# Splitting a weight transfer by tile, and moving the issue of attention's value loads

## The chip, the core and the metric

The kernel runs on one core of a Trainium2 chip. The metric is device time in microseconds (us), the median of several executions. The engines are TensorE (PE; PEld is its weight loads), VectorE (DVE), ScalarE (ACT), GpSimd (POOL) and SyncE (SP), which here issues all transfers from one queue, in order.

## What is computed

The result is a gated mix, `g * a + (1 - g) * b`, of an attention branch with memory and a gated feed-forward branch, over the same 2048 rows of 576 columns.

```python
x = A_x
g = _sigmoid((x * gate_w).sum(-1, keepdims=True))
a = _A_ref(x, A_wq, A_wk, A_wv, A_wo, A_beta)
b = _B_ref(x, B_w_gate, B_w_up, B_w_down)   # (gelu(x @ w_gate) * (x @ w_up)) @ w_down, F = 4608
return g * a + (1 - g) * b
...
for s in range(N):                          # N = 4 segments of 512 rows, 32 heads of 18
    logits = jnp.einsum("bhqd,bhkd->bhqk", qs, ks) * scale + mask
    a_dot = jnp.einsum("bhqk,bhkd->bhqd", _softmax(logits), vs)
    num = jnp.einsum("bhld,bhde->bhle", phi(qs), M)
    den = jnp.einsum("bhld,bhd->bhl", phi(qs), z)[..., None] + 1e-6
    outs.append(g * num / den + (1.0 - g) * a_dot)
    M = M + jnp.einsum("bhld,bhle->bhde", phi(ks), vs)
    z = z + jnp.einsum("bhld->bhd", phi(ks))
```

## The kernel before

The kernel holds each operand as a pair of float16 words, high and low, scaled by a power of two that is formed from sums of squares; most products are three matmuls. It has three stages.

**Projections.** The 2048 rows are four chunks of 512 (`s` or `c`, 0 to 3). The 576 columns of x are five tiles (`KT`; the fifth is a half tile). For each chunk nine column tiles of q and k (`project`, L329 in `chain_w`), and the value rows for four blocks of 128 rows (`vrows`, L339 in `chain_x`) are formed. They go to DRAM: q and k as `qk` from `stage` buffers, of which there are three (L485), values as `vp` (L510).

The first chunk's values don't wait for any scale: `first_words` (L527) multiplies the raw float32 x by the raw float32 value weights `raw_v`. The weights' 578 columns are two halves, `VB`: 288 columns (`NH`) and 290 (two more hold the mix's gate weight). For the first half all four row blocks are formed for k = 0 to 4, in the PSUM banks dn, dn, V and pv; for the second half row blocks 0 and 1 (banks G and U), then 2 and 3 (both st). `raw_v` and the raw q and k weights lie in memory that later is the accumulator `acc`, and so have that name in the trace.

Before and between these matmuls stand the sums that give the scales. `scale_x(0)` sums the squares of x, made by ACT (L154), with matmuls (L160), and reduces them on DVE (L162 to L169). `stat_v` sums the squares of each value tile, both halves, on DVE (L81). `scale_v` adds these with a matmul (L90) and so do the q and k sums later (`stat_qk`, on DVE L81 and ACT L431, then `scale_sum(0, ..)`, a second L90). With x's scale ACT makes high words (L175) and DVE low words (L180, L185).

**Attention and feed-forward together.** 72 steps (`step`) each take one of 36 tiles of 128 hidden columns for one pair of chunks; four steps make a block `fb`, the place in it is `i4`. `weights_load` issues the loads of gate and up words (`load_g`, L205, `raw`) and of down words (`load_d`, L211, `rawd`), four or five tiles ahead. In steps 2 to 65 a head of attention is worked on beside it: scores (L909), their maximum on DVE, powers and high words on ACT, low words on POOL, a transpose by DMA from `ph` to `pt` (L945), and the products with the values (`values`, L959). `load_v` (L882) loads the values of four heads as `vt`, of which there are two buffers.

**Tail.** The output projection and the mix.

The order on PE, DVE, ACT and POOL is that in which the code is written (`manual_schedule`). SP's order is chosen by the scheduler from what each transfer waits for. Transfers complete on eight lanes taken in turn (`DMAHW0` to `DMAHW7`); a transfer waits for the one before it on its lane, unless a wait before has covered that. The framework finds the waits between a transfer and its readers from the memory that each of them spans.

Of the kernel before, what the change touches and what calls it, by code (L numbers as in the profile page):

```python
# [24 lines left out]
NH = D // 2  # L25
KT = 5
# [16 lines left out]
def kernel(ctx: ExitStack, tc: tile.TileContext, xs, wqk, wv, wo, wgu, wd, beta, out):  # L43
    nc = tc.nc
    pe, act, dve, pool, sp = nc.tensor, nc.scalar, nc.vector, nc.gpsimd, nc.sync
# [19 lines left out]
    def flat(ap):  # L65
        return ap.rearrange("p a b -> p (a b)") if len(ap.shape) == 3 else ap

    def raw_tile():
        return wts.tile([P, 2 * KT * P], F32, name="raw", tag="raw", bufs=3)
# [72 lines left out]
    def load_first(raw_v):  # L142

        x_raw[0] = []
        x_sq[0] = flat(wts.tile([P, 2, GB * P], F16, name="pairg", tag="pairg", bufs=2)).bitcast(BF16)
        for k in range(KT):
            if k % 2 == 0:
                x_raw[0].append(raw_tile())
            sp.dma_start(x_raw[0][-1][:, (k % 2) * L : (k % 2 + 1) * L], xs[0, :, k])
            sp.dma_start(raw_v[:, k, :NH], wv[:, k, :NH])  # L150
        sp.dma_start(raw_v[:, :, NH:], wv[:, :, NH:])

    def square_x(c, k):
        act.activation(x_sq[c][:, k * L : (k + 1) * L], x_raw[c][k // 2][:, (k % 2) * L : (k % 2 + 1) * L], AF.Square)  # L154
# [47 lines left out]
    def load_g(f):  # L202
        if f < NF:
            raw_g[f] = raw_tile()
            sp.dma_start(raw_g[f], flat(wgu[f]))  # L205

    def load_d(f):
        if f >= NF:
            return
        raw_d[f] = home["r"].tile([P, D], F32, name="rawd", tag="rawd", bufs=2)  # L210
        sp.dma_start(raw_d[f], wd[f])  # L211
# [195 lines left out]
    with tc.tile_pool(name="prj", bufs=2, side="right", reuse_waits="tile") as pp:  # L407
# [12 lines left out]
        raw_v = kept["words"][:, : KT * (D + 2)].rearrange("p (k c) -> p k c", k=KT)  # L420
# [186 lines left out]
        with tc.manual_schedule(engines=ORDERED):  # L607
# [4 lines left out]
            for _ in range(30):  # L612
                pe.matmul(start[:, :P], onesb, onesb, start=True, stop=True)
            load_first(raw_v)
            for g in range(5):
                load_qk(g)
# [234 lines left out]
    with tc.tile_pool(name="keep", bufs=2, side="right", reuse_waits="tile") as kp, ExitStack() as tail:  # L851
# [25 lines left out]
        def load_v(gg):  # L877
            if gg >= H // 2:
                return
            hf, g = divmod(gg, H // 4)  # L880
            vts[gg] = ap_.tile([P, 8, 4 * VC], F16, name="vt", bufs=2)
            sp.dma_start(vts[gg], vps[hf][:, g * 4 * VC : (g + 1) * 4 * VC].rearrange("(t p) c -> p t c", p=P))  # L882
# [102 lines left out]
        def result_low(gg):  # L985
            hf, g = divmod(gg, H // 4)
            ob, oh = obs.pop(gg), ohs.pop(gg)
            dve.scalar_tensor_tensor(flat(oh[:, 1]), flat(ob), wsc[:, 3:4], flat(oh[:, 0]), OP.mult, OP.subtract)
            d0 = g * 4 * DH
            for i in range(2):  # L990
                for a, b, c in ((d0, min(d0 + 4 * DH, 4 * P), i * 4 * P), (max(d0, 4 * P), d0 + 4 * DH, (4 + i) * P - i * 64)):
                    if a < b:
                        sp.dma_start(oas[hf][:, c + a : c + b].rearrange("(t p) c -> p t c", p=P),
                                     oh[:, i, :, a - d0 : b - d0])
# [87 lines left out]
        def weights_load(fb, i4):  # L1082
            n0 = 2 * fb
            if i4 == 1:
                load_g(n0 + 4)
            if i4 == 2:
                load_d(n0 + 2)
            if i4 == 3:
                load_g(n0 + 5)
                if not fb:  # L1090
                    load_d(n0 + 3)
            if i4 == 0 and fb > 1:
                load_d(n0 + 1)
# [34 lines left out]
        def step(v):  # L1128

            f, p = divmod(v, 2)  # L1130
            fb, i4 = divmod(v, 4)
            c, e = 2 * p, 2 * p + 1
            k = v - LAG
# [56 lines left out]
            if fb:  # L1190
                weights_high(fb, i4)
                weights_low(fb, i4)
            weights_load(fb, i4)
            product(V, f, A22, x2_, 0, 4)
            rest(V, f, G4, x1, (0,) if fb else (0, 1))
# [82 lines left out]
            load_head(k + 2)  # L1278
            if done == H // 2 - 1:
                result_low(done)  # L1280
            if i4 == 0:
                load_v(fb)
            if i4 == 2:
                load_ob(fb)

# [31 lines left out]
        with tc.manual_schedule(engines=ORDERED):  # L1317
            for v in range(2 * NF):
                step(v)

                if v == LAST:
                    atn.close()
                    op_ = tail.enter_context(tc.tile_pool(name="outp", bufs=2, side="right", reuse_waits="tile"))
                if v >= LAST:
                    turned(2 * (v - LAST))
                    turned(2 * (v - LAST) + 1)
                    if v < LAST + 2:
                        finish(v - LAST)
# [4 lines left out]
            fb = NB - 1  # L1333
# [54 lines left out]
```

## Time and profile before

| | |
|---|---|
| time, median of 3 runs (lowest to highest) | 1606.44 us (1605.73 to 1607.4) |
| the profiled execution: time, span | 1604.73 us, 1603.0 us |
| mean granted TensorE clock | 0.998 |
| PE, DVE, ACT, POOL busy | 99%, 70%, 73%, 71% |
| moved by SP's queue | 206.92 MB, 71.6% of 16 DMA engines' time |

A busy time is an average over the stages. A wait is the idle time just before an instruction, with the instruction that ended last among those it waited for; a row of waits gives the sum, how often, and the longest. A chain row gives start, length and what ran. In a timeline row the start and the length come first, and the idle time before it, if any, stands last in brackets.

### The profile page before, as it was taken

To read this page: it belongs to the slowest core of one execution; us is meant where nothing else is said; L and a number is where in the kernel's file an instruction comes from. 1 tells how busy PE (TensorE), PEld (TensorE's weight loads), DVE (VectorE), ACT (ScalarE), POOL (GpSimd) and SP (SyncE) were. 2 spreads that over 40 slices of the span, in tenths; PEclk is the share of its full clock that TensorE was granted. 3 is DMA by queue.
4 is the path that set the end of the run, shared out by engine and by line. 5 is a ranking of instruction groups with operands and counts; after the bars stand their busy time and mean duration, and the time that the engine had idled before them with its cause. 6 is when DMAs were issued, how large, how long until landed. Compare 5 with 4: busy or idle time off the path is not lost.

```text
span 1603.0 us, 32556 instructions
## 1 busy us (share of the span) xinstructions
PE 1585.7 (99%) x11914; PEld 934.8 (58%) x11914; DVE 1117.5 (70%) x2938; ACT 1163.2 (73%) x1968; POOL 1134.0 (71%) x1093
## 2 busy tenths in 40 slices
PE   7999999999999999999999999999999999999999
PEld 5556654555555555555555555555555555555577
DVE  5755785777777777777777777677777777766643
ACT  4765554989888887879888888878798888864200
POOL 2231557788988888887979788888879797886300
PEclk9999999999999999999999999999999999999999
DMA  5632343879787887979797987989798979846241
GB/s 199 221 108 81 134 144 89 133 126 149 128 131 137 123 137 129 137 119 156 124 145 129 133 142 123 139 129 144 119 159 131 139 130 131 135 75 149 66 133 60
DMA packets 473248, 209.00 MB, mean 130 GB/s; under 512 B 427648, under 2 KB 438400, under 8 KB 472576
## 3 DMA queue, kind: packets, MB, share of 16 engines
q1 hardware_dynamic: 473088, 206.92, 71.6%
q8 instruction: 94, 1.54, 0.4%
q14 instruction: 66, 0.54, 0.1%
HBM read 90.99 MB, written 27.26 MB: 74 GB/s over the span
## 4 chain that ended last, share of the span: by engine, by line
PE 90%; ACT 3%; DMA 3%; POOL 2%; DVE 1%; issue 1%; SPq 0%; ACTq 0%; POOLq 0%; DVEq 0%
PE dn L1004 24%; PE U L1044 16%; PE V L1044 11%; PE G L1044 11%; PE pv L959 4%; PE st L339 3%; PE st L329 2%; PE dn L339 2%; PE U L1050 2%; PE G L329 2%; DMA pt<-ph 2%; PE G L1055 1%; PE V L1055 1%; PE st L909 1%; PE U L329 1%; PE G L1050 1%
## 5 line engine op out<-in xcount | busy, mean ns | idle before, releaser
L1004 PE MATMUL dn<-paird,hh 128*128 128x288 f16 x3396 | 485.4, 286 | 0.0
L939 POOL TENSOR_TENSOR ph<-pf,ph 128x512 f16<-128x512 f32 (+1 forms) x256 | 354.1, 1405 | 170.0 <-ACT ph L938 169.9
L1044 PEld LDWEIGHTS <-pairg 128*128 128x128 f16 x3024 | 279.8, 98 | 269.0 <-issue 18.3
L1004 PEld LDWEIGHTS <-hh 128*128 128x128 f16 x3456 | 338.0, 98 | 155.3 <-issue 0.2
L1012 DVE SCALAR_TENSOR_TENSOR acc<-dn,ev,acc 128x288 f32<-128x288 f32 x534 | 274.6, 515 | 69.0 <-PE dn L1004 68.7
L928 ACT ACTIVATE pf<-pf,mb,esc 128x512 f32<-128x512 f32 (+3 forms) x512 | 293.2, 644 | 7.0 <-POOL ph L939 0.4
L1044 PE MATMUL G<-x,pairg 128*128 128x512 f16 x864 | 220.9, 379 | 0.0
L1044 PE MATMUL U<-xt,pairg 128*128 128x512 f16 x864 | 210.0, 379 | 0.0
L1031 POOL TENSOR_TENSOR hh<-gl,hh 128x512 f16<-128x512 f32 x144 | 164.1, 1160 | 38.7 <-ACT hh L1030 38.7
L310 POOL TENSOR_TENSOR pairg<-raw,pairg 128x640 f16<-128x640 f32 (+2 forms) x144 | 174.5, 1235 | 12.9 <-ACT pairg L306 12.9
L938 ACT ACTIVATE ph<-pf 128x512 f16<-128x512 f32 (+1 forms) x256 | 172.7, 722 | 0.0
L306 ACT ACTIVATE pairg<-raw 128x640 f16<-128x640 f32 (+2 forms) x144 | 90.2, 653 | 107.9 <-POOL raw L300 56.0
L1198 DVE COPY gl<-U 128x512 f32<-128x512 f32 x72 | 49.8, 692 | 160.3 <-PE U L1044 157.4
L915 DVE CUSTOM_DVE_ANT_0 pf<-st,mask 128x512 f32<-128x512 f32 (+1 forms) x256 | 157.5, 616 | 0.0
L275 POOL TENSOR_SCALAR raw<-raw,sc 128x640 f32<-128x640 f32 x72 | 134.9, 1887 | 0.0
L1044 PE MATMUL U<-x,pairg 128*128 128x512 f16 x432 | 127.1, 379 | 0.4 <-DVE gl L1221 0.4
L1034 ACT ACTIVATE gl<-gl,sc 128x512 f32<-128x512 f32 x144 | 96.7, 716 | 41.8 <-DVE gl L1225 29.1
L915 DVE CUSTOM_DVE_ANT_0 pf<-dn,mask 128x256 f32<-128x256 f32 (+1 forms) x256 | 80.8, 354 | 60.5 <-PE dn L909 60.5
L1030 ACT ACTIVATE hh<-gl 128x512 f16<-128x512 f32 x144 | 85.9, 621 | 31.8 <-DVE gl L1026 31.3
L1044 PE MATMUL V<-xt,pairg 128*128 128x512 f16 x432 | 105.7, 381 | 0.0
L1044 PE MATMUL V<-x,pairg 128*128 128x512 f16 x432 | 104.8, 378 | 0.0
L959 PEld LDWEIGHTS <-pt 128*128 128x128 f16 x2560 | 78.4, 96 | 23.4 <-issue 16.3
(270 smaller groups left out, 2513.9 us busy)
## 6 DMA issues: line engine op xcount, KB each, us to landing
raw<-in_wgu_dram SPq DMA_DIRECT2D x36, 640.0 KB
rawd<-in_wd_dram SPq DMA_DIRECT2D x36, 288.0 KB
qk<-stage SPq DMA_DIRECT2D x36, 256.0 KB
qt<-qk SPq DMA_DIRECT2D x128, 72.0 KB
kt<-qk SPq DMA_DIRECT2D x128, 72.0 KB
vp<-vstage SPq DMA_DIRECT2D x16, 296.0 KB
vt<-vp SPq DMA_DIRECT2D x16, 296.0 KB
qt<-qk SPq DMA_DIRECT2D x128, 36.0 KB
```

Source lines behind the costliest of these rows:

```text
L275: pool.tensor_scalar(r, r, scl[f // 2][0][:, 0:1], None, OP.mult)
L310: pool.tensor_tensor(spot(f, *p, 1), raw_g[f][:, p[0] : p[1]], spot(f, *p, 0), OP.subtract)
L915: dve.tensor_tensor_reduce(prob[a][:, COL[qi] : COL[qi + 1]], ov, mask[:, L - (qi + 1) * P :], 1.0, -3e38, OP.add, OP.max, mx[a][:, qi : q ...
L928: act.activation(r, r, AF.Exp, bias=b[:, qi : qi + 1], scale=esc[:, 0, c : c + 1])
L938: act.activation(h[:, 0, cols], p[:, cols], AF.Copy)
L939: pool.tensor_tensor(h[:, 1, cols], p[:, cols], h[:, 0, cols], OP.subtract)
L959: pe.matmul(ov, pr[:, 10 * i + COL[qi] // P + kb], v[:, 4 * e + kb, c0 : c0 + VC], start=kb == 0 and i == 0, stop=kb == qi and i == 1)
L1004: pe.matmul(o[:, :NH], hh[:, a, q * P : (q + 1) * P], w[:, b, n * NH : (n + 1) * NH], start=i == 0, stop=i == 5)
L1012: dve.scalar_tensor_tensor(av, o[:, :NH], ev, av, OP.mult, OP.add)
L1031: pool.tensor_tensor(hh[:, 1], t, hh[:, 0], OP.subtract)
L1034: act.activation(t, o, AF.Gelu_apprx_tanh, scale=scl[f // 2][0][:, 2 + c : 3 + c])
L1044: pe.matmul(o, w[:, i, (a + k) * P : (a + k + 1) * P], x[:, b + k], start=start and n == 0, stop=n == 5, skip_group_check=True)
```

## The change

There are two edits. In `load_first` the second halves of the value weights are loaded by five transfers, one for each tile, where one transfer brought all five. In `weights_load` the values of the next block of four heads are asked for at `i4 == 3`, ahead of the gate and up words; in `step` they were asked for at the end of the step with `i4 == 0`. The first values stay where they were, at the end of step 0.

```diff
@@ load_first
-        sp.dma_start(raw_v[:, :, NH:], wv[:, :, NH:])
+        for k in range(KT):
+            sp.dma_start(raw_v[:, k, NH:], wv[:, k, NH:])
@@ weights_load
             if i4 == 3:
+                load_v(fb + 1)
                 load_g(n0 + 5)
@@ step, its end
-            if i4 == 0:
-                load_v(fb)
+            if v == 0:
+                load_v(0)
```

SP's order at the start, from the last first half on, before (`acc<-in_wv_dram` are the value weights, `acc<-in_wqk_dram` those of q and k, `raw<-in_xs_dram` tiles of x; in brackets the semaphores that are waited for):

```order
L149 DMA raw<-in_xs_dram 128x512 [waits DMAHW0_49]
L150 DMA acc<-in_wv_dram 128x288 [waits DMAHW1_49]
L426 DMA acc<-in_wqk_dram 128x2x640 [waits DMAHW2_49]
L151 DMA acc<-in_wv_dram 128x5x290 [waits DMAHW5_49,DMAHW7_49,DMAHW3_49,DMAHW1_49]
L426 DMA acc<-in_wqk_dram 128x2x640 [waits DMAHW4_49]
```

and with the change:

```order
L149 DMA raw<-in_xs_dram 128x512 [waits DMAHW0_49]
L150 DMA acc<-in_wv_dram 128x288 [waits DMAHW1_49]
L152 DMA acc<-in_wv_dram 128x290 [waits DMAHW2_49]
L152 DMA acc<-in_wv_dram 128x290 [waits DMAHW3_49]
L152 DMA acc<-in_wv_dram 128x290 [waits DMAHW4_49]
L152 DMA acc<-in_wv_dram 128x290 [waits DMAHW5_49]
L152 DMA acc<-in_wv_dram 128x290 [waits DMAHW6_49]
L427 DMA acc<-in_wqk_dram 128x2x640 [waits DMAHW7_49]
```

The second halves now stand ahead of all q and k weights, and wait for lanes alone; before, the one transfer waited for four first halves. On PE the order stays, and the second halves' matmuls wait for their own tile's lane.

Further on, in the projections of the first chunk, SP's order before (`acc<-in_xs_dram` are 1 MB loads of x for later sums, `qk<-stage` stores of q and k):

```order
L485 DMA qk<-stage 128x2x512 [waits DMAHW3_49,DVE_49,Activation_49]
L356 DMA acc<-in_xs_dram 128x2048 [waits DMAHW4_49,DVE_49]
L356 DMA acc<-in_xs_dram 128x2048 [waits DMAHW5_49,DVE_49]
L485 DMA qk<-stage 128x2x512 [waits DMAHW6_49,DVE_49]
L485 DMA qk<-stage 128x2x512 [waits DMAHW7_49,DVE_49,Activation_49]
```

and with the change:

```order
L486 DMA qk<-stage 128x2x512 [waits DMAHW7_49,DVE_49,Activation_49]
L357 DMA acc<-in_xs_dram 128x2048 [waits DMAHW0_49,DVE_49]
L486 DMA qk<-stage 128x2x512 [waits DMAHW1_49,DVE_49]
L357 DMA acc<-in_xs_dram 128x2048 [waits DMAHW2_49,Activation_49]
L486 DMA qk<-stage 128x2x512 [waits DMAHW3_49,DVE_49,Activation_49]
```

One store stands between the two loads now. In attention, at the third load of values, SP's order before:

```order
L945 DMA_TRANSPOSE pt<-ph 128x10x128 [waits DMAHW1_49,Pool_49]
L205 DMA raw<-in_wgu_dram 128x1280 [waits DMAHW2_49,Pool_49]
L211 DMA rawd<-in_wd_dram 128x576 [waits DMAHW3_49,Pool_49]
L882 DMA vt<-vp 128x8x148 [waits DMAHW4_49]
L871 DMA qt<-qk 36x1x1024 [waits DMAHW5_49,PE_49]
```

and with the change:

```order
L946 DMA_TRANSPOSE pt<-ph 128x10x128 [waits DMAHW5_49,Pool_49]
L883 DMA vt<-vp 128x8x148 [waits DMAHW6_49]
L206 DMA raw<-in_wgu_dram 128x1280 [waits DMAHW7_49,Pool_49]
L212 DMA rawd<-in_wd_dram 128x576 [waits DMAHW0_49,Pool_49]
L872 DMA qt<-qk 36x1x1024 [waits DMAHW1_49,PE_49]
```

The load of the values has passed one load of gate and up words and one of down words.

## The prediction, made before the changed kernel ran

> **What bounds the kernel now.** I read the busy times first, then what TensorE (PE) waited for, then the chain of waits through the first 60 us, and last the start's timeline.
>
> ```profile
> span 1603.0 us, 32556 instructions
> ...
> PE 1585.7 (99%) x11914; PEld 934.8 (58%) x11914; DVE 1117.5 (70%) x2938; ACT 1163.2 (73%) x1968; POOL 1134.0 (71%) x1093
> ...
> PE dn L527 <- DMA acc<-in_wv_dram: 8.0, 1, 8.0
> PE pv L959 <- DMA pt<-ph: 3.1, 4, 1.6
> PE dn L341 <- DVE x L185: 1.4, 1, 1.4
> ```
>
> PE is busy for all but 17 us. An edit that only moves transfers can gain what PE idles, and time in which PE works at a lower clock. The largest idle piece is one wait of 8.0 us on the values' weights, the transfer that the change splits. The chain of waits shows where (start, length):
>
> ```profile
> 9.90 4.65 DMA acc<-in_wv_dram
> ...
> 14.68 2.26 PE dn L527 x4
> ...
> 18.63 1.08 PE st L160 x5
> 19.71 0.97 PE dn L527 x4
> ```
>
> The second halves' one transfer is issued only at 9.90 us, when all first halves have landed, and lands at 14.55. The group at 14.68 is k = 1 of the *first* halves, whose own words were there long before. It takes 2.26 us where the equal group at 19.71 takes 0.97. The stretches (length; PE, PEld, DVE, ACT, POOL busy; granted clock; DMA share; GB/s) say why:
>
> ```profile
> 4.00:5.00 1.00, 1.00 (x8) 0.92 (x6) 0.00 (x0) 0.15 (x1) 0.86 (x3) 1.00 0.80 214
> 6.00:10.00 4.00, 0.65 (x3) 0.19 (x1) 0.00 (x0) 2.06 (x4) 1.96 (x7) 1.00 1.02 368
> 12.00:18.00 6.00, 3.32 (x7) 2.49 (x8) 3.17 (x9) 0.00 (x0) 0.00 (x0) 0.50 1.04 394
> ```
>
> Up to 10 us the granted clock is full, though PE stops at 6.65; after some 5 us of idleness it is at half, and stays there to 18 us.
>
> **Part 1, the split at the start.** Two things follow from the built program. There PE's k = 1 matmuls ask for the *second* completion of lane DMAHW3 before (the big transfer, twelfth in the queue; lanes go round by eight) and for the first one now (their own words). Each of the five new transfers waits only for the one eight places ahead, as the order of SP shows, and the q and k weights move behind them. PE's second-half matmuls get a wait per tile.
>
> Removed: PE's wait from the end of k = 0 to 14.68. These rows of the timeline give the new course (start, length):
>
> ```profile
> 0.78 0.39 SPq L149 DMA_DIRECT2D raw<-in_xs_dram  x1
> ...
> 3.52 0.63 ACT L154 ACTIVATE pairg<-raw 128x512 bf16<-128x512 f32 x1 [1.45 <-DMA raw<-in_xs_dram]
> ...
> 5.66 0.39 SPq L426 DMA_DIRECT2D acc<-in_wqk_dram  x1
> ...
> 6.00 0.65 PE L527 MATMUL pv<-acc,raw 128*128 128x288 f32 x2
> ...
> 6.90 0.63 ACT L154 ACTIVATE pairg<-raw 128x512 bf16<-128x512 f32 x1 [0.60 <-DMA raw<-in_xs_dram]
> ...
> 8.41 0.63 ACT L154 ACTIVATE pairg<-raw 128x512 bf16<-128x512 f32 x1 [0.88 <-DMA raw<-in_xs_dram]
> ...
> 9.51 0.63 ACT L154 ACTIVATE pairg<-raw 128x512 bf16<-128x512 f32 x1 [0.47 <-DMA raw<-in_xs_dram]
> ...
> 17.91 0.76 DVE L81 CUSTOM_DVE_ANT_0 junk<-acc 128x578 bf16<-128x578 f32 x1
> ...
> 19.75 0.69 DVE L162 TENSOR_REDUCE x<-st 128x1 f32<-128x512 f32 x1 [1.07 <-PE st L160]
> ...
> 21.23 2.80 ACT L175 ACTIVATE x<-raw,xsc 128x1024 f16<-128x1024 f32 x3 [11.09 <-DVE xsc L168]
> ...
> 30.14 0.23 ACT L431 ACTIVATION_READ_ACCUMULATOR krow<-acc 128x1 f32 x1
> ...
> 31.66 0.28 PE L90 MATMUL dn<-wst,ones 128*128 128x9 f32 x2
> ...
> 32.94 1.55 ACT L108 ACTIVATE wp<-acc,wsc 128x640 f16<-128x640 f32 x2 [1.18 <-DVE wsc L99]
> ```
>
> *PE's own course.* k = 0 ends at 6.65; k = 1 takes 1.9 us at full clock (the 0.97 of two row blocks, and again for the other two), to 8.6. The sums of x's squares (L160) then wait for the last square on ScalarE (ACT), 9.51 + 0.63 = 10.14; the last of five costs 1.08/5 = 0.22, so they end at 10.36 instead of 19.71: 9.35 us sooner. An idle of 1.5 us is short beside the 5 us that went ahead of the clock's fall, so I take full clock. If nothing else held it, PE would reach the sum for the q and k scale (L90) 9.35 sooner, at 22.3.
>
> *The weights' landing.* By 6.0 us 1.06 MB had moved (177 GB/s over those 6 us). Until the last second half lands 2.79 MB must: five x tiles of 256 KB, five first halves of 144 KB, 725 KB of second halves:
>
> ```profile
> 0.00:6.00 6.00, 4.81 (x37) 4.50 (x37) 0.00 (x0) 2.24 (x3) 5.05 (x26) 1.00 0.63 177
> ...
> raw<-in_xs_dram SPq DMA_DIRECT2D x8, 256.0 KB
> acc<-in_wv_dram SPq DMA_DIRECT2D x1, 725.0 KB
> acc<-in_wv_dram SPq DMA_DIRECT2D x5, 144.0 KB
> ```
>
> The other 1.73 MB take 4.7 us at 368 GB/s and 8.1 at 214 (the slowest full microsecond): 10.7 to 14.1. The fifth transfer also waits for x's fourth tile, 8.41, and a transfer in an empty queue took 3.52 - 0.78 = 2.74, so not before 11.2. I take 12.0, the mean rate of 291, as these are rows of 1.1 to 2 KB like the ones of 4 to 5 us.
>
> *DVE and ACT behind it.* VectorE (DVE) has all five sums of squares of the weights ahead of x's scale. The last ends 0.85 after landing, 12.85; the scale takes 21.23 - 19.75 = 1.5; ACT's conversions start at 14.35 instead of 21.23, 6.9 sooner. ACT then had no gap up to 30.37, so it ends that piece at 23.5, and L90, which asks for ACT's last sum, comes 1.2 after PE is ready for it: 31.66 - 23.55 = **8.1 us sooner**. With landing at 14.1 ACT is 4.8 sooner and the 1.29 of slack it had (31.66 - 30.37) makes 6.1; with 11.2 it is 9.0. The stall thus moves: next late is ACT, not the weights. The rest hangs on L90: ACT's L108 had 1.18 us idle and follows L90's result as before. The q and k weights, 2.95 MB at the 394 of 12 to 18 us, land by 19.5, about when DVE wants the last; ACT wants them later.
>
> Added: four more issues on SP at 0.39 us (the rows L149 and L426), 1.6 us, hidden, since SP sat waiting from 6.05 (the end of L426's row) to 9.90. Uncovered they would cost 1.6 once.
>
> [...]
>
> **Behind the start.** In SP's order the fourth stage (qk) transfer now stands ahead of the third of the 1 MB loads of x (L356), where it stood behind two in a row.
>
> ```profile
> 53.96 7.94 DMA qk<-stage
> ...
> 62.01 0.60 ACT L472 ACTIVATE stage<-st 128x512 f16<-128x512 f32 x1 [4.06 <-DMA qk<-stage]
> ```
>
> It took 7.94 us in the chain (first row), ACT idled 4.06 for it (second, of the timeline), and PE its 1.4 us at L341 behind that. One megabyte (1.05 million bytes) less ahead of it is 2.7 us at 394 GB/s, more than 1.4: I count **1.4**, with 0 as the low end.
>
> **Part 2, the values' load in attention.** It is fifteen times the same. SP's scheduled order moves it past two loads, not by a step, as the scheduler had pulled it forward before:
>
> ```profile
> 357.22 0.38 SPq L205 DMA_DIRECT2D raw<-in_wgu_dram  x1
> ...
> 358.87 0.43 SPq L882 DMA_DIRECT2D vt<-vp  x1
> ...
> 377.67 0.72 ACT L85 ACTIVATE junk<-raw 128x640 bf16<-128x640 f32 x1
> ```
>
> The values come 1.65 us sooner, which nobody waits for (L882 is in no wait). The gate and up words, and the down words behind them, go out 0.5 us later; they are read first at 377.67, 20 us behind the issue. The load waits for no engine: the transposes ahead of it have already waited for PE. **Zero**; uncovered 15 x 0.5 = 7.5 us.
>
> **Sum.** 8.1 + 1.4 = 9.5 us. The profiled execution took 1604.73 (span 1603.0 and 1.73 around it), so 1595.2; the median of the runs lies 1.71 above it: **1596.9**. Ends: 6.1 + 0 gives 1600.3, 9.0 + 1.4 gives 1596.0.
>
> **Rivals.**
> 1. *The five transfers land one after the other.* If each takes 1.5 us (8.41 - 6.90) behind the last first half (9.9, as the big transfer's wait ended), the last lands at 17.4. ACT is then 1.4 sooner, L90 2.7, in all 4.1: **1602.3**. For: the slowest microsecond, 214 GB/s, fell among these small rows. Against: 368 GB/s right behind it, with eight transfers open.
> 2. *Given back in the next chunk.* Two of the 1 MB loads now stand behind stage transfers, x's next tiles behind them. If both came onto the path at 2.7 us each, 5.3 of 9.5 go: **1602.2**. Against: the DMA engines had nothing to do from 20 to 32 us (row below), so the whole piece can slide forward.
>
> ```profile
> 20.00:32.00 12.00, 12.00 (x56) 8.74 (x55) 8.57 (x26) 10.53 (x25) 0.00 (x0) 1.00 0.01 1
> ```
>
> 3. *Slower: SP is held at the values' load.* If it blocked until its buffer is free, the words, heads and transposes behind it would go late, and PE would wait at L959 for pt. One wait as long as the longest there, 1.6 us, in each of 15 groups is 24 us: **1621**. From 0.63 us a group (9.5/15) on the change loses. For: SP is one queue in order, and pt is waited for four times. Against: the load's only wait is a lane.
> 4. *It doesn't do what it says.* If something else still held k = 1 until all weights are there, little would change: **1606.4**, the median. For: one wait can stand for several. Against: the built program asks for these words' own completion alone.
>
> **How the numbers follow.** Forecast 0.76; rival 1 0.08, rival 2 0.08, rival 3 0.05, rival 4 0.03. Rivals 1 and 2 gain about 4.1 and 4.2 us, a microsecond beyond the 0.2% (3.2 us) that a measurement tells from no change, so I put a third of their chance to no change: faster 0.87, same 0.08, slower 0.05. The forecast's own range is 1596.0 to 1600.3; with 1.5 us below for the spread of the runs (1605.73 to 1607.4) and for what my bounds miss, and reaching to rivals 1 and 2 above, it is 1594.5 to 1602.5.
>
> **What would show it.** PE's wait on the values' weights gone and k = 1 at 6.7; clock 1.0 from 2 to 34 us; ACT's conversions (L175) near 14.4 and L90 near 23.5, with a PE wait there of about 1 us on ACT; the first projection (L329 in the old lines) at 26.6 instead of 34.69; no wait at x's last low words. In attention the same four waits for pt. It is wrong if the last second half lands after 14.1, if the clock still falls, or if a wait of microseconds appears between 30 and 310 us.

## The result, and the profile after

The changed kernel took 1596.08 us (median of 4 runs, 1594.94 to 1597.19) beside 1606.09 us of the kernel before (4 runs, 1605.59 to 1607.4). The ratio is 0.9936, with a 95% interval of 0.9919 to 0.9954: about 10.0 us, 0.6%, faster. The prediction said 1596.9. The number came out; the sum behind it did not, as three of its terms were off and made up for each other.

The profiled execution of the changed kernel took 1594.94 us, its span 9.8 us less than before. First the page: the span, and the busy times of the engines.

```profile
span 1593.2 us, 32558 instructions
...
PE 1585.4 (100%) x11914; PEld 934.2 (59%) x11914; DVE 1116.6 (70%) x2938; ACT 1162.3 (73%) x1968; POOL 1132.8 (71%) x1093
```

Then the view of PE's waits (line waited for: us in total, times, longest):

```profile
PE dn L90 <- ACT krow L432: 2.0, 1, 2.0
PE G L614 <- POOL onesb L610: 1.2, 1, 1.2
PE st L161 <- ACT pairg L155: 0.5, 1, 0.5
PE U L1045 <- DVE gl L1223: 0.4, 1, 0.4
PE pv L960 <- DMA pt<-ph: 0.2, 1, 0.2
```

PE is busy for 1585.4 us, as it was before (1585.7), so what went is idle time. (The half clock of before is gone, but it held PE's work for some 3.6 us, from 14.68 to about 18.3, and a new slow stretch of about as much work, shown below, makes up for it.) The listed waits sum to 14.1 us before (8.0, 3.1 and 1.4, and two that both kernels have, 1.2 at L613 and 0.4 at L1044) and to 4.3 now. Gone are the 8.0 on the values' weights, the 1.4 at x's low words, and 2.9 of the 3.1 on `pt`. New are 2.0 at L90, on ACT's last sum of squares, and 0.5 at L161.

The timeline of the start shows the new course (start, length; idle time ahead in brackets; the lines are one further on than before):

```profile
5.77 2.65 SPq L152 DMA_DIRECT2D acc<-in_wv_dram  x5
...
6.47 1.16 PE L528 MATMUL dn<-acc,raw 128*128 128x288 f32 x4
...
9.92 0.38 PE L161 MATMUL st<-pairg,onesb 128*128 128x512 bf16 x1 [0.45 <-ACT pairg L155]
...
10.14 0.76 DVE L81 CUSTOM_DVE_ANT_0 junk<-acc 128x578 bf16<-128x578 f32 x1 [10.14 <-DMA acc<-in_wv_dram]
...
13.36 0.76 DVE L81 CUSTOM_DVE_ANT_0 junk<-acc 128x578 bf16<-128x578 f32 x1
...
14.04 0.69 DVE L163 TENSOR_REDUCE x<-st 128x1 f32<-128x512 f32 x1
...
15.52 2.19 ACT L176 ACTIVATE x<-raw,xsc 128x1024 f16<-128x1024 f32 x2 [5.65 <-DVE xsc L169]
...
24.42 0.23 ACT L432 ACTIVATION_READ_ACCUMULATOR krow<-acc 128x1 f32 x1
...
24.71 0.39 PE L90 MATMUL dn<-wst,ones 128*128 128x9 f32 x2 [2.02 <-ACT krow L432]
24.95 4.58 PE L528 MATMUL st<-acc,raw 128*128 128x290 f32 x12
29.46 2.76 PE L330 MATMUL G<-x,wp 128*128 128x512 f16 x12
```

k = 1 of the first halves runs at 6.47 instead of 14.68. The five transfers are issued in 2.65 us; DVE's first sum starts at 10.14, and between its first and its fifth (10.14 and 13.36) it waits for nothing: (13.36 - 10.14)/4 = 0.80 us for each sum with the short read behind it. So the second to fifth tiles were there when DVE came to them. ACT starts its conversions (L176) at 15.52 instead of 21.23, PE's L90 comes at 24.71 instead of 31.66, and the first projection (L330) at 29.46. The group before it, twelve matmuls, takes 4.58 us. The view of stretches says why (length; PE, PEld, DVE, ACT, POOL busy; granted clock; DMA share; GB/s):

```profile
2.00:18.00 16.00, 15.54 (x82) 11.59 (x80) 7.41 (x26) 5.69 (x9) 5.58 (x17) 1.00 0.99 343
...
24.00:25.00 1.00, 0.29 (x3) 0.29 (x3) 0.00 (x0) 1.00 (x4) 0.00 (x0) 1.00 0.68 221
25.00:26.00 1.00, 1.00 (x4) 0.71 (x5) 0.73 (x6) 1.00 (x4) 0.00 (x0) 0.53 0.59 238
26.00:27.00 1.00, 1.00 (x4) 0.71 (x3) 0.66 (x5) 0.95 (x3) 0.70 (x3) 0.50 0.00 0
...
28.00:29.00 1.00, 1.00 (x5) 0.47 (x5) 0.97 (x2) 0.00 (x0) 0.69 (x1) 0.76 0.22 83
```

From 2 to 18 us the clock is now full and the DMA engines have work throughout. But it falls to half at about 25.0 us, right behind PE's 2.02 us of idleness, and is back at about 28.5.

One more pair of rows splits the gain between the start and attention: the products of attention with the values, in the view of the tile `pt` (count, least/median/most ns of one, start of the first and of the last). Before:

```profile
L959 PE MATMUL pv<-vt,pt x2560: 178/178/193, 286.2 to 1441.0; 128*128 128x37 f16 x197
```

and with the change:

```profile
L960 PE MATMUL pv<-vt,pt x2560: 177/179/193, 279.6 to 1430.9; 128*128 128x37 f16 x197
```

The first product comes 6.6 us sooner. That is the 5.2 us of the first projection, which started at 34.62 in the trace of before, and the 1.4 of the low words. From the first product to the last it takes 1151.3 us instead of 1154.8: attention itself, which the prediction counted at zero, gave 3.5, of which 2.9 are the waits for `pt`. Behind the last product the change is 0.3 longer, so 6.6 + 3.5 - 0.3 is the span's 9.8.

### The profile page after: what moved, and what is told of

It is laid out like the page before. It is cut to its first block, busy times and chain, and to the rows that moved or that the text cites. A ratio compares the mean times of both kernels' runs of the same rounds, so it can differ in the third digit from the quotient of the medians.

```text
span 1593.2 us, 32558 instructions
## 1 busy us (share of the span) xinstructions
PE 1585.4 (100%) x11914; PEld 934.2 (59%) x11914; DVE 1116.6 (70%) x2938; ACT 1162.3 (73%) x1968; POOL 1132.8 (71%) x1093
## 4 chain that ended last, share of the span: by engine, by line
PE 96%; ACT 2%; DMA 1%; issue 1%; DVE 0%; POOL 0%; SPq 0%; ACTq 0%; DVEq 0%
PE dn L1005 26%; PE U L1045 17%; PE V L1045 12%; PE G L1045 11%; PE pv L960 4%; PE st L340 3%; PE st L330 3%; PE dn L340 2%; PE U L1051 2%; PE G L330 2%; PE G L1056 1%; PE V L1056 1%; PE U L330 1%; PE st L910 1%; PE G L1051 1%; PE V L1051 1%
```

## The experiments

Three things had to be told apart: what each of the two edits is worth, why the waits for `pt` went, and what the wait at L90 and the fallen clock cost. The letters in the expectations name the theories told there. Each edit alone, the first run of scale first and the filler ran on one chip beside a kernel before of 1604.59 us; fewer values, half the filler, the change again and scale first again ran on another beside 1605.24. So times of the two groups are compared by their ratios.

**Each edit alone.** The split alone puts the values' load back:

```diff
@@ weights_load
-                load_v(fb + 1)
@@ step, its end
-            if v == 0:
-                load_v(0)
+            if i4 == 0:
+                load_v(fb)
```

> The split of the second halves alone; the values' load in attention as before. The profile of the change gave 9.8 us of span: 5.2 up to the first projection (29.46 instead of 34.62), 1.4 at x's last low words, and 2.9 from the waits for pt (3.1 before, 0.2 after), which the prediction had counted as zero. Theory A (the values' load, out of the way of the transposes, took those 2.9): waits for pt of about 3 us as before, start as in the change, time about 1606.1 - 6.6 = 1599.5. Rival B (they went with the start's shift, or come and go from run to run): waits for pt of 0.3 or less, time about 1596.

It took 1599.97 us, ratio 0.9969 (0.9959 to 0.9979). Its waits of PE:

```profile
PE pv L960 <- DMA pt<-ph: 4.0, 8, 1.3
PE dn L90 <- ACT krow L432: 2.0, 1, 2.0
```

and its row of the products:

```profile
L960 PE MATMUL pv<-vt,pt x2560: 178/178/193, 279.9 to 1436.7; 128*128 128x37 f16 x197
```

The start is that of the change: the same 2.0 us at L90, the first product at 279.9, no wait at the low words. The waits for `pt` are back, and attention takes 1156.8 us: of the 6.3 us by which the first product comes sooner than before, attention gives back 2.0.

The moved load alone has the change's `load_v` and the one transfer for all second halves:

```diff
@@ load_first
-        for k in range(KT):
-            sp.dma_start(raw_v[:, k, NH:], wv[:, k, NH:])
+        sp.dma_start(raw_v[:, :, NH:], wv[:, :, NH:])
```

> The values' load alone moved; the second halves in one transfer as before. Theory A: the start as before (8.0 us wait, first projection at 34.6), waits for pt 0.3 or less instead of 3.1, time about 1603.2. Rival B: waits for pt about 3, time 1606 as before.

It took 1602.11 us, ratio 0.9979 (0.997 to 0.9987). Its waits of PE:

```profile
PE dn L527 <- DMA acc<-in_wv_dram: 7.3, 1, 7.3
...
PE pv L959 <- DMA pt<-ph: 0.3, 1, 0.3
PE dn L341 <- DVE x L185: 0.3, 1, 0.3
```

and its row of the products:

```profile
L959 PE MATMUL pv<-vt,pt x2560: 178/178/193, 285.8 to 1437.1; 128*128 128x37 f16 x197
```

The start has its long wait again, and attention takes 1151.3 us, just as in the change. So each edit alone makes the kernel faster, the moved load by some 2.5 us (1604.59 - 1602.11) and the split by some 4.6, and the load's gain lies in attention. Together they give more than these 7.1 us, since the split alone loses 2.0 in attention.

Two things don't fit what came before. The wait at x's low words is 0.3 here, with SP's order at the start as it was before, where it was 1.4. ACT waits 2.90 us for the `qk` store there where it waited 4.06, so PE's wait and ACT's are shorter by the same 1.2 us. So that much of the 1.4 may be how late one store landed in one profile, and not the order in which the 1 MB loads go out; why it landed sooner stays open. And the clock falls sooner in the long wait. PE's k = 0 ends at 7.33 here, and one row of stretches already has less than full clock:

```profile
9.00:10.00 1.00, 0.00 (x0) 0.00 (x0) 0.00 (x0) 0.63 (x1) 0.00 (x0) 0.70 1.04 409
```

From 10 to 12 the mean is 0.50. If the clock was full and then half in the row shown, its 0.70 puts the fall at about 9.4, 2.1 us after PE stopped (an estimate from these means). In the trace of before it was 4.8 us by the same estimate: k = 0 ended at 6.65, and the stretch from 11 to 12 has 0.72, those from 9 to 11 have 1.00.

**Fewer values.** If it is the traffic of the values that makes `pt` late, and not the earlier start or chance, then a kernel that has the split alone and hardly loads values must lose the waits without any load being moved. This kernel, on top of the split alone, leaves out the loads from the third group of heads on and multiplies with the first two groups' values instead, so that part of the result is left out:

```diff
@@ load_v
+            if gg >= 2:
+                vts[gg] = vts[gg - 2]
+                return
```

> The split alone, and 14 of the 16 loads of the values in attention left out: the groups from the third on multiply with the first two groups' values, so that part of the result is left out of the computation. Theory A (the 296 KB of values, queued behind gate, up and down words, stand ahead of the transposes that PE waits for): waits for pt 0.6 us or less instead of 4.0, time like that of the whole change, about 3 us under the split alone. Rival G (it is the gate, up and down words' own place in the queue, 0.5 us sooner or later, that counts): waits for pt about 3 to 4 us, time as with the split alone.

It took 1595.43 us, ratio 0.9942 (0.993 to 0.9955), and attention 1151.5 us. Its wait for `pt`:

```profile
PE pv L963 <- DMA pt<-ph: 0.5, 1, 0.5
```

and the row of the products:

```profile
L963 PE MATMUL pv<-vt,pt x2560: 178/178/193, 279.8 to 1431.3; 128*128 128x37 f16 x197
```

Without 14 of the 16 loads attention is as short as with the loads moved (1151.3), and the start is the same. The gate, up and down words go out where they did before in this kernel, so their own place in the queue is not what counts. So the loads of the values, where they stood before, are what delayed the transposes. The timeline shows where that was, at one block. Before, SP and then PE:

```profile
646.40 1.34 SPq L945 DMA_TRANSPOSE pt<-ph  x1
648.87 0.37 SPq L205 DMA_DIRECT2D raw<-in_wgu_dram  x1
650.11 0.35 SPq L211 DMA_DIRECT2D rawd<-in_wd_dram  x1
650.52 0.43 SPq L882 DMA_DIRECT2D vt<-vp  x1
...
652.43 5.16 SPq L945 DMA_TRANSPOSE pt<-ph  x2
...
661.84 0.64 PE L959 MATMUL pv<-vt,pt 128*128 128x37 f16 x19 [1.62 <-DMA pt<-ph]
```

and with the change:

```profile
641.13 0.76 SPq L883 DMA_DIRECT2D vt<-vp  x1
642.29 0.35 SPq L206 DMA_DIRECT2D raw<-in_wgu_dram  x1
643.53 0.34 SPq L212 DMA_DIRECT2D rawd<-in_wd_dram  x1
...
645.49 4.22 SPq L946 DMA_TRANSPOSE pt<-ph  x2
```

Before, the gate, up, down and value words (640, 288 and 296 KB, as the page's rows of issues have them) went out within 2.1 us of each other, the values last, 1.9 us ahead of the transposes. SP had sat idle ahead of the first two of them (from 647.74 to 648.87 and from 649.24 to 650.11), which wait for POOL. Now the values go into that idle time, 4.4 us ahead of the transposes, and SP is busy with the two transposes for 4.22 us where it was 5.16. PE waited 1.62 us for `pt` here before; in this profile of the change it nowhere waits longer than 0.2 for it. What it is in the loads of the values that delays the transposes, their bytes or something else, was not shown. Nor is the distance in the queue all that counts, as the filler below shows.

**Scale first.** The wait at L90 hangs on ACT, ACT on x's scale, and x's scale on five sums of DVE that x's scale doesn't use. This kernel, on top of the change, forms x's scale behind the first of them, and PE multiplies the first half's last tile ahead of the weights' scale:

```diff
-            for k in range(KT):
-                stat_v(k)
+            stat_v(0)
...
             scale_x(0)
+            for k in range(1, KT):
+                stat_v(k)
             for k in range(2, 4):
                 first_words(va, 0, k, range(4))
-            scale_v()
             first_words(va, 0, 4, range(4))
+            scale_v()
```

> The change, and DVE forms x's scale behind the first of the five weights' sums instead of behind all five; PE does the first half's last words ahead of the weights' scale. Theory C (the start is now paced by DVE's five sums and, behind x's scale, by ACT): x's scale about 3 us sooner (12.4 instead of 15.5), ACT's last sum near 21.6, no wait of PE at the second L90, first projection near 26 instead of 29.5, time about 1592.5. Rival D (the landing of the q and k weights, or PE itself, holds that piece): first projection moves by less than 1 us, time 1595 to 1596.

It took 1594.08 us, ratio 0.9929 (0.9916 to 0.9941). Rows of its timeline:

```profile
12.50 2.80 ACT L176 ACTIVATE x<-raw,xsc 128x1024 f16<-128x1024 f32 x3 [2.45 <-DVE xsc L169]
...
22.74 0.28 PE L90 MATMUL dn<-wst,ones 128*128 128x9 f32 x2
22.88 2.89 PE L528 MATMUL st<-acc,raw 128*128 128x290 f32 x12
25.70 3.01 PE L330 MATMUL G<-x,wp 128*128 128x512 f16 x12
```

ACT starts 3.0 us sooner than in the change, L90 waits for nothing, the twelve matmuls take 2.89 us, and the first projection comes 3.76 us sooner: 2.0 of idleness and 1.7 of clock. The time is less clear than the trace: 1592.5 was expected, and the ratio lies within the interval of the change's 0.9936 (0.9919 to 0.9954).

**Filler.** To tell these two apart, 34 matmuls of constants (128x128, into the bank of the sum) stand ahead of the second L90. They add no result and keep PE busy over the wait:

```diff
-    def sums(st):
+    def sums(st, fill=0):
+        o = spare()
+        for _ in range(fill):
+            pe.matmul(o[:, :P], onesb, onesb, start=True, stop=True)
...
-        dve.tensor_reduce(t, sums(st), AX.X, OP.add)
+        dve.tensor_reduce(t, sums(st, 34 * (i == 0)), AX.X, OP.add)
```

> The change, and 34 matmuls of 128x128 of ones into the sum's own bank ahead of the second L90, so that PE has work in the 2.0 us in which it waits for ACT; they compute nothing that is kept. Theory E (the 2.0 us of idleness drop the clock to half from 25.0 to 28.6 us): granted clock 1.0 throughout 22 to 32 us, the 12 matmuls behind L90 take 2.9 instead of 4.6, first projection near 27.8 instead of 29.5, time about 1.7 less, 1594.4. Rival F (the clock falls at this point whatever PE does): clock 0.5 there as before, no change or a little slower.

```profile
22.89 2.06 PE L91 MATMUL dn<-onesb 128*128 128x128 bf16 x34
...
24.99 2.89 PE L531 MATMUL st<-acc,raw 128*128 128x290 f32 x12
27.81 2.76 PE L333 MATMUL G<-x,wp 128*128 128x512 f16 x12
```

It took 1594.26 us, ratio 0.9928 (0.9914 to 0.9942). The twelve matmuls start when they did with the change and take 2.89 us instead of 4.58; the first projection comes at 27.81 instead of 29.46. Here the clock stays full without the idleness, and that is worth 1.7 us.

Its profiled execution, of 1597.03 us, was the longest of its five. Attention took 1155.1 us there, and of the 2.3 us waited for `pt` 2.0 fell in one wait:

```profile
726.57 0.64 PE L963 MATMUL pv<-vt,pt 128*128 128x37 f16 x19 [1.98 <-DMA pt<-ph]
```

The load of the values had gone out at 712.12, 4.4 us ahead of the transposes at 716.49, just as in the block of the change above; SP was busy with these two for 6.02 us all the same. So the moved load makes these waits rarer, but not impossible, and what held the transposes here stays open. The stretches behind this wait show the clock falling once more:

```profile
729.00:730.00 1.00, 1.00 (x6) 0.65 (x5) 0.00 (x0) 0.00 (x0) 0.48 (x1) 0.50 0.13 46
```

The means are 0.70 from 727 to 728, 0.50 to 730, and 0.59 to 731, which puts half clock at about 727.4 to 730.8 (an estimate from these means). The 1.62 us that PE idled for `pt` before 661.84 in the trace of before left the clock full: every microsecond from 660 to 668 has 1.00.

**Half the filler, and both kernels again.** To see whether the clock stays full behind a shorter idle time, 17 matmuls were put there in place of 34:

```diff
-        dve.tensor_reduce(t, sums(st, 34 * (i == 0)), AX.X, OP.add)
+        dve.tensor_reduce(t, sums(st, 17 * (i == 0)), AX.X, OP.add)
```

> The change, and 17 filling matmuls instead of 34 ahead of the second L90, so that PE idles about 1.0 us there instead of 2.0 (nothing that they compute is kept). If the clock falls for any idle stretch of a microsecond: half clock for some 3.5 us behind it, first projection at 29.4, time as the change. If it takes nearer to the 2.0 us that dropped it: clock 1.0, first projection at 27.8, about 1.6 us less than the change.

It took 1594.48 us, ratio 0.9937 (0.9924 to 0.9951). The clock stayed full (1.00 in every stretch from 22 to 30 us), but the run does not settle the question: the weights had landed later in it (PE waited 0.5 us for the values' weights), the fillers themselves waited 0.44 us for DVE, and only some 0.5 us of idleness was left on either side of them. The 1.62 us of before, behind which the clock stayed full, and the 1.98 of the filler, behind which it fell, both in attention, stand closer together; but each is one observation, and in the next run the clock stayed full behind 2.02 us.

The change once more:

> The change itself once more, beside the others on the same chip. Theory A: waits for pt small again, 0.0 to 1 us in all; ratio to before 0.993 to 0.995. Rival B (they come and go by chance): 3 us or more in one such profile.

It took 1596.47 us, ratio 0.9944 (0.9932 to 0.9957). Its profiled execution surprised:

```profile
24.82 0.39 PE L90 MATMUL dn<-wst,ones 128*128 128x9 f32 x2 [2.02 <-ACT krow L432]
25.07 2.89 PE L528 MATMUL st<-acc,raw 128*128 128x290 f32 x12
27.89 2.76 PE L330 MATMUL G<-x,wp 128*128 128x512 f16 x12
```

The same 2.02 us of idleness, at the same place, and the clock stays full (1.00 in every stretch from 22 to 30 us, 2.89 us for the twelve). This execution was the fastest of its five, 1593.45 us. In the three other profiles with that wait (the change's first, the split alone, fewer values) the clock fell: the twelve take 4.58, 4.53 and 4.53 us. So it falls in some executions and not in others, and the full clock of a single filler profile could be chance. The mean granted clock of every execution is on record and speaks against that. A stretch of 3.5 us at half takes 0.0011 off the mean (3.5 x 0.5/1593.2). Of the 22 executions of kernels with the 2.02 us wait (the change's nine, the split alone, fewer values) 14 have 0.999 or less. Of the twenty without it (both runs of scale first, both fillers) 19 have 1.000; the other is the filler's profiled one, with its fall at 727.

The waits for `pt` are small again: none is among its listed waits, and attention takes 1151.0 us. Over all traces, attention takes 1154.8 and 1156.8 us with the values' load in its old place, and 1151.0 to 1152.3 with the load moved, but for the filler's 1155.1.

Scale first once more, beside it:

> The version with x's scale behind the first weights' sum once more, so that it stands beside the change on one chip. Theory C: its first projection starts 3.8 us sooner (25.70 and 29.46 in the profiles), 2.5 to 3.5 us less time than the change. Rival: what it gains at the start is given back later, less than 1 us.

It took 1592.63 us (1592.44 to 1593.78), ratio 0.9925 (0.9913 to 0.9938): the median is 3.8 us below the change's on the same chip, and the mean of five 3.0. Of the change's five executions only the one just shown lies within its range; four lie above, and the two intervals overlap only from 0.9932 to 0.9938. So it is faster than the kernel before, and very likely than the change. Its first projection came at 26.66 this time, not at 25.70. Its profile shows what holds PE next, in PE's waits and in a row of the timeline:

```profile
PE dn L90 <- DVE vstage L508: 0.6, 1, 0.6
```

```profile
22.03 0.82 DVE L81 CUSTOM_DVE_ANT_0 junk<-acc 128x640 bf16<-128x640 f32 x1 [1.26 <-DMA acc<-in_wqk_dram]
```

PE waits for DVE, 0.6 us here and 0.3 more at L330 for the scaled weights. But DVE itself came late to the first of these because it had waited 1.26 us for weights of q and k. With x's scale out of the way, the landing of these weights comes onto the path.

## Why the prediction was right, and where it was wrong

**Right.** The split takes the 8.0 us wait away and the half clock with it; k = 1 was put at 6.7 and came at 6.47. The last square's sum was to end at 10.36 and ended at 10.30 (9.92 + 0.38). PE was to be ready for the second L90 at 22.3 and was at 22.69 (24.71 - 2.02). The transfers did not land one after the other at 1.5 us each, which would have put the last at 17.4: all five had landed by 13.36, when DVE took the last without waiting. L90 then waited for ACT, as the prediction named it, and the low words' 1.4 us went. Nothing was given back in the next chunk (the first product of attention came 6.6 us sooner, 5.2 + 1.4), and SP was not held at the values' load (0.2 us for `pt` in all).

**Wrong: DVE behind the landing.** "The last ends 0.85 after landing, 12.85" took DVE to be done with four sums when the fifth tile lands. The first tile was there only at 10.14, and from then on five sums of 0.80 us set the pace, not the landing: x's scale started at 14.04. The term is 1.2 too early: conversions at 15.52 for 14.35, ACT's last sum at 24.65 for 23.5, L90 at 24.71 for 23.55. PE's wait there grew from the 1.2 forecast to 2.0. Scale first, which takes four of the sums out of that chain, shows it: ACT started at 12.50.

**Wrong: the clock.** "An idle of 1.5 us is short beside the 5 us that went ahead of the clock's fall, so I take full clock" made a bound out of one observation. That the clock still falls was among the prediction's own signs of being wrong. The idle time became 2.0 at another place, the second L90, and behind it the clock fell in three of four profiles; with the moved load alone, in the very wait that the 5 was read from (8.0 us before, 7.3 there), it fell after some 2.1. The 1.5 itself was not refuted, as 1.62 once left the clock full. The fall cost 4.58 - 2.89 = 1.7 us, as the filler shows. With the 1.2 of DVE, that takes the first term from 8.1 to the 5.2 measured.

**Wrong: part 2 at zero.** The prediction asked who waits for the values, found nobody, and forecast the same four waits for `pt`. The question to ask was what waits behind them in the queue. The waits for `pt` went from 3.1 us to 0.2, and attention took 3.5 us less; the moved load alone and the kernel with fewer values show that the load was the cause, though the filler's profile shows that moving it doesn't rule such a wait out. It had stood in the trace of before: SP's rows at 648.87 to 652.43 end in the transposes whose result PE waited for.

So the span's 9.8 us are 5.2 at the start, 1.4 at the low words and 2.9 at `pt` (sum 9.5), where the prediction had 8.1, 1.4 and 0 (sum 9.5). The forecast time was right by luck: the first term, too large by 2.9 for two reasons, met one that was too small by as much. The 1.4 was right in size; its cause, one megabyte less ahead of a store, is in doubt, since the moved load alone had only 0.3 there with the old order. So 1.2 of it may be a matter of when one store landed.

## What to carry to other kernels

When a wait is taken away, walk through the engines behind it for the rate at which they take their work, not only for when the last piece lands: here five sums of 0.80 us, none of them needed by the scale behind them, became the pace, and reordering them took another 3 to 4 us off where it was measured beside the change (1.1 by the ratios of the first run of each). A load that nobody waits for can still delay a later transfer that somebody does wait for (here the waits for `pt` were 3.1 us with the load in its old place and 0.2 with it moved); cost a moved transfer by what stands behind it in the queue and by the idle time of the queue that it moves into. A new wait on PE should be priced with the clock as well as with its own length: here one of 2.02 us cost some 1.7 us more in three of four profiles.

## What the hardware showed that was not expected

The granted clock fell to half behind 2.02 us of idleness of PE, in three of four profiles that have this wait, and in that of the change it stayed there for about 3.5 us of work; the twelve matmuls behind it took 4.53 to 4.58 us instead of 2.89. In the fourth it did not fall. It fell behind 1.98 us in the filler's profile, and not behind 1.62 in the profile of before. In the wait of the moved load alone it fell after some 2.1 us, and in that of before after some 4.8. Why it fell in some executions and not in others is not shown.
